# A spectral layer and an FFN in float32: the first DFT of batches 3 to 7 with high and low x stacked on the contraction rows

## The chip, the cores and the metric

One core of a Trainium2 chip runs the whole program. The metric is the device time of one execution in microseconds. The engines are TensorE (PE in the profile, with its weight loads as PEld), VectorE (DVE), ScalarE (ACT), GpSimd (POOL) and SyncE (SP), which issues all DMAs of this kernel in the order of its queue.

## The reference

The input x is 8 x 3008 x 256. Along the sequence of 3008 a real FFT is taken, each frequency is multiplied by a complex 256 x 256 matrix with a bias, real and imaginary parts are shrunk towards zero by 0.01, and the inverse FFT goes back to the sequence. The 24064 rows that result go through an FFN with 2048 hidden units and g = h - tanh(h).

```
X = rfft(x, axis=1);  Xr, Xi = X.real, X.imag
Yr = Xr @ w_r - Xi @ w_i + b_r;  Yi = Xr @ w_i + Xi @ w_r + b_i
Yr, Yi = sign(Y) * max(abs(Y) - 0.01, 0)      # each of the two
y = irfft(Yr + 1j * Yi, n=3008, axis=1).reshape(24064, 256)
h = y @ w_in;  out = (h - tanh(h)) @ w_out
```

## The kernel before

**Accuracy.** A float32 operand is split into a high part, rounded to the format that TensorE multiplies (F32R), and the low remainder. A product is then three matmuls: low matrix by high data, high by high, high by low, added up in one PSUM bank. The high part is a cast on ACT, the low part a subtraction on POOL or DVE (`split_into`, lines 86 to 89; its two operations carry the lines L87 and L88 in the profile).

**The spectral part, batch by batch.** 3008 = 47 x 64, so the FFT falls into two. The *first DFT* is over 47 points for all 64 residues, which are 32 *pairs* of two: a pair has 94 rows (2 x 47) and 256 channels, and the table f1 (94 x 96) holds the 47-point table twice, one block for each residue of the pair. `Forward` loads four pairs, splits two at a time (`split`), multiplies them (`dft`, three matmuls with 94 contraction rows and 512 columns, L216 to L218), copies the bank out (`keep`, L230) and stores four pairs to an intermediate in DRAM (`a_dram`). The *second DFT* (`Spectrum`) reads the intermediate in another order (`load`, tile `at`), transforms it (`dft`), multiplies it with the 256 x 256 matrices (`shared`, `cross`), adds (`join`), shrinks and transforms back (`inverse`, tile `zo`), and stores it to `z_dram`. A `Unit` loads up to four pairs of that (tile `zin`) and makes the last inverse DFT with the table i2, which lies whole in SBUF (L428); its result goes to the tile `raw`, the input of the FFN.

**The FFN.** The tokens go by in 48 chunks (six a batch) of 512 or 480. From chunk 3 on, each chunk is eight `Pair`s of two blocks of 128 hidden units. The first layer is a Strassen-like scheme with seven products of half size, whose operands (t3, b11, t2, b21, t1, b22, t4; tiles y_t, y_b, y_more) are sums and splits made once a chunk on ACT and POOL (`sums`, `operands`). A pair has the PSUM tile H: products in four phases, a sum on DVE between phase 1 and 2 (`u3`, L611) and one after phase 2 (`low_right`, L617), then tanh on ACT (L626), h - tanh(h) on DVE (`g`, L629), the split (L633, L637), and the second layer (`down`, L524).

**Order.** The program is written out by hand: each engine runs its instructions in the order in which the code makes them. The main loop goes over the pairs, two *slots* a pair, sixteen a chunk, 96 a batch. `plan()` puts the spectral steps into slots: `put(slot, rank, fn)`, and in a slot the lower rank goes first. What a step returns is run a little later in the same or the next slot (`run_later`, `run_last`). With zs as the slot of a batch's first chunk, the second DFT of batch b has its twelve steps at zs - 89, zs - 83 and so on, six slots apart, each with its products two, three and seven slots later, and its load seven slots ahead. The sixteen steps of the first DFT go, from batch 2 on, into the calmest slots between zs - 113 and zs - 94 (`calmest`), a place where the second DFT of the batch before has ended and its own has not begun; each step is split one slot ahead. Two PSUM banks (tag `f`) serve all spectral steps in turn, and the tiles of the splits (tags `sp_h`, `sp_l`, two buffers each) serve the first DFT, the second and the shrunk result.

## Time and profile before

| | |
|---|---|
| median of 3 runs | 2632.07 us (2631.01 to 2635.33) |
| the profiled execution | 2638.48 us |
| its span, first to last instruction | 2636.7 us |
| mean granted TensorE clock | 0.995 |
| DMA | 163.88 MB, mean 62 GB/s |

The profile is one execution, 6.4 us above the median. Its page gives the busy time of each engine over the span, the chain of waits that ended last, and the costliest groups of instructions by line, with the mean duration of one and the idle time ahead of it. Stretches, groups, waits and the order in time can be asked of the trace. The steady state begins near 500 us, and a batch then takes 318 us.

### The profile page before, as it was taken

What the parts mean: (1) busy time and instruction counts of PE and PEld (TensorE: products, weight loads), DVE (VectorE), ACT (ScalarE), POOL (GpSimd) and SP (SyncE); (2) the same over time, 40 slices, a digit from 0 to 9 for tenths busy, and PEclk for the clock granted to TensorE, in tenths of its full rate; (3) what the DMA queues carried; (4) which work ended last, traced back from release to release, by engine and by line L of the source; (5) the groups of instructions that cost most, each with busy time, mean ns of one, the idle gap of its engine ahead of it and who ended that gap; (6) DMA issues with size and microseconds to landing.
All of it is one profiled execution on the core that took longest, in us unless ns stands there. A gap on an engine that the chain in (4) does not pass through costs nothing.

```text
span 2636.7 us, 43245 instructions
## 1 busy us (share of the span) xinstructions
PE 2604.5 (99%) x16641; PEld 2344.8 (89%) x16641; DVE 1728.6 (66%) x2612; ACT 1571.5 (60%) x2870; POOL 695.5 (26%) x830
## 2 busy tenths in 40 slices
PE   8999999999999999999999999999999999999999
PEld 6787888899989999899998999999999999999998
DVE  6787775676656667566665667656665667665655
ACT  5555656655576555755666555665556655565655
POOL 0002524322252222412223222332223322221210
PEclk9999999999999999999999999999999999999999
DMA  6520323211131111411114011231112211111000
GB/s 194 153 76 15 112 68 99 66 51 40 47 104 59 48 46 38 119 47 40 46 48 128 29 55 39 80 88 42 42 53 85 69 46 54 36 33 33 16 25 16
DMA packets 104653, 163.88 MB, mean 62 GB/s; under 512 B 8000, under 2 KB 62272, under 8 KB 104352
## 3 DMA queue, kind: packets, MB, share of 16 engines
q1 hardware_dynamic: 104448, 161.13, 20.1%
q8 instruction: 131, 2.15, 0.4%
q14 instruction: 74, 0.61, 0.1%
HBM read 86.13 MB, written 74.97 MB: 61 GB/s over the span
## 4 chain that ended last, share of the span: by engine, by line
PE 92%; issue 2%; POOL 2%; DVE 2%; DMA 1%; ACT 1%; POOLq 0%; SPq 0%; ACTq 0%; DVEq 0%
PE o L524 37%; PE H L595 32%; PE ps_v L289 4%; PE ps_i L428 4%; PE ps_f L262 3%; PE ps_t L289 2%; PE he L500 2%; PE ps_v L371 1%; PE ps_f L218 1%; PE ps_f L216 1%; PE ps_f L217 1%; DVE y L326 1%; PE oe L524 1%; PE ps_i L336 1%; PE ps_i L337 1%
## 5 line engine op out<-in xcount | busy, mean ns | idle before, releaser
L595 PEld LDWEIGHTS H<-y_t,sum 128*128 128x128 f32 x3240 | 531.3, 189 | 86.9 <-POOL y_t L88 1.4
L633 ACT CAST gh<-th 128x1024 fp32r<-128x1024 f32 (+1 forms) x360 | 372.3, 1034 | 362.5 <-DVE th L629 268.0
L524 PE MATMUL o<-gh,wout_l 128*128 128x512 f32 (+1 forms) x1440 | 568.5, 395 | 0.1
L524 PE MATMUL o<-gl,wout_h 128*128 128x512 f32 (+1 forms) x1440 | 560.2, 389 | 0.5 <-DVE gl L637 0.5
L524 PE MATMUL o<-gh,wout_h 128*128 128x512 f32 (+1 forms) x1440 | 559.8, 389 | 0.0
L595 PE MATMUL H<-y_t,sum 128*128 128x256 f32 (+1 forms) x3240 | 551.0, 278 | 1.4 <-ACT ot L535 0.7
L637 DVE TENSOR_TENSOR gl<-th,gh 128x1024 fp32r<-128x1024 f32 (+1 forms) x360 | 441.3, 1226 | 58.1 <-ACT gh L633 54.4
L629 DVE TENSOR_TENSOR th<-H,th 128x1024 f32<-128x1024 f32 (+1 forms) x360 | 429.4, 1193 | 3.8 <-ACT th L626 1.4
L611 DVE TENSOR_TENSOR H<-H,late 128x256 f32<-128x256 f32 (+1 forms) x360 | 153.5, 426 | 417.9 <-PE H L595 373.9
L626 ACT ACTIVATE th<-H 128x1024 f32<-128x1024 f32 (+1 forms) x360 | 364.4, 1012 | 105.5 <-PE H L595 101.9
L524 PEld LDWEIGHTS o<-gl,wout_h 128*128 128x128 f32 x1440 | 270.9, 188 | 55.3 <-DVE gl L637 0.9
L617 DVE TENSOR_TENSOR H<-H,late 128x256 f32<-128x256 f32 (+1 forms) x360 | 153.6, 427 | 248.6 <-PE H L595 241.6
L88 POOL TENSOR_TENSOR z_l<-mn,z_h 128x512 fp32r<-128x512 f32 x84 | 110.7, 1318 | 741.4 <-ACT z_h L87 741.4
L595 PE MATMUL H<-y_b,win_h 128*128 128x256 f32 (+1 forms) x1440 | 286.4, 279 | 0.5
L524 PEld LDWEIGHTS o<-gh,wout_l 128*128 128x128 f32 x1440 | 272.2, 189 | 9.1 <-DVE ot L537 1.1
L524 PEld LDWEIGHTS o<-gh,wout_h 128*128 128x128 f32 x1440 | 271.9, 189 | 6.7
L595 PE MATMUL H<-y_more,win_h 128*128 128x256 f32 (+1 forms) x1440 | 267.4, 279 | 0.4 <-POOL y_more L88 0.4
L603 ACT COPY late<-H 128x256 f32<-128x256 f32 (+1 forms) x360 | 132.8, 369 | 222.1 <-PE H L595 218.3
L595 PEld LDWEIGHTS H<-y_more,win_h 128*128 128x128 f32 x1440 | 220.0, 189 | 5.9 <-POOL y_more L88 0.6
L595 PEld LDWEIGHTS H<-y_b,win_h 128*128 128x128 f32 x1440 | 219.6, 189 | 1.7 <-POOL y_b L88 1.7
L595 PE MATMUL H<-y_more,win_l 128*128 128x256 f32 (+1 forms) x720 | 206.4, 287 | 0.5 <-DVE H L617 0.5
L595 PE MATMUL H<-y_b,win_l 128*128 128x256 f32 (+1 forms) x720 | 200.1, 278 | 0.0
(176 smaller groups left out, 4177.5 us busy)
## 6 DMA issues: line engine op xcount, KB each, us to landing
xt<-in_x SPq DMA_DIRECT2D x64, 384.0 KB, 3.8
at<-a SPq DMA_DIRECT2D x96, 256.0 KB, 3.2
z<-zo SPq DMA_DIRECT2D x96, 256.0 KB, 2.1
a<-st SPq DMA_DIRECT2D x56, 384.0 KB, 3.2
zin<-z SPq DMA_DIRECT2D x49, 384.0 KB, 4.3
out<-ot SPq DMA_DIRECT2D x32, 512.0 KB, 3.1
out<-ot SPq DMA_DIRECT2D x16, 480.0 KB, 3.0
w_raw<-in_moe_w_in SPq DMA_DIRECT2D x8, 512.0 KB, 6.4
```

The costliest lines, as they stand in the source:

```text
L88: rest.tensor_tensor(out=lo, in0=src, in1=hi.bitcast(F32), op=ALU.subtract)
L289: nc.tensor.matmul(dst, lhs[:, t], rhs[:, t, :], start=n == 0, stop=n == 5)
L428: nc.tensor.matmul(ps[:, at + j * 94:at + (j + 1) * 94], self.zt[:, k, t * P:(t + 1) * P], i2t[:, (self.p + k) * 94:(self.p + k + 1) * 94] ...
L524: nc.tensor.matmul(self.o[t][:, :n], lhs[:, f, t * P:(t + 1) * P], rhs, start=f == 0 and k == 0, stop=f == NF - 1 and k == 2,)
L595: nc.tensor.matmul(dst, a, b, start=start and k == 0, stop=k == 2, skip_group_check=True)
L603: nc.scalar.copy(out=self.p7, in_=self.c11)
L611: nc.vector.tensor_tensor(out=self.c21, in0=self.acc, in1=self.p7, op=ALU.add)
L617: nc.vector.tensor_tensor(out=self.c22, in0=self.acc, in1=self.p7, op=ALU.add)
L626: nc.scalar.activation(out=self.th, in_=self.hp[:, :, :n], func=AF.Tanh)
L629: nc.vector.tensor_tensor(out=self.th, in0=self.hp[:, :, :self.n], in1=self.th, op=ALU.subtract)
L633: nc.scalar.copy(out=self.gh, in_=self.th)
L637: nc.vector.tensor_tensor(out=self.gl, in0=self.th, in1=h(self.gh), op=ALU.subtract)
```

## The change

For batches 3 to 7 the first DFT is done by a new class, `Stacked`, on one pair of 512 columns after another. x comes in a second layout, `x_twice`, which the host writes: a pair has both residues side by side (2 x 256 columns), on rows 0 to 46 and again on rows 64 to 110. Both copies are cast on ACT; on rows 64 to 127 the cast is then replaced by the low part, for the first pair of a step on POOL, for the second on DVE. So one operand of 128 rows has high x above and low x below. The table f1s has the high matrix against both, which gives 48 output rows, and the low matrix against high x, which gives 48 more. One matmul a pair does what three did for two pairs, so a step of two pairs has two matmuls into two banks. The two groups of 48 rows are not added in PSUM: they are stored to two intermediates (`a_dram[b][0]` and `[1]`), both are loaded by the second DFT, and POOL adds the second to the first (`fix`) ahead of the transform.

The steps are no longer crowded together: they stand six slots apart, between the steps of the second DFT of the batch before, and the last three four slots apart. A step is split two slots ahead, at the end of the slot.

The table i2 is given up after the first units. Its space in SBUF, a tile named `shared`, then holds two pieces of the table, which each unit loads for itself, two buffers for the second intermediate, and every third load of `x_twice`.

```diff
     f1 = np.zeros((94, 96))
     f1[:47, :48] = one
     f1[47:, 48:] = one
+    f1s = np.zeros((128, 96))
+    f1s[:47, :48] = f1s[:47, 48:] = f1s[64:111, :48] = one
     n1 = np.array([2 * pair + par for par in range(2) for pair in range(NP)])
     th = 2 * np.pi * np.outer(n1, np.arange(128) % 64) / 64
     c, s = np.cos(th).reshape(2, NP, 128), np.sin(th).reshape(2, NP, 128)
...
             i2[par, 0, :, pair, par] = w * np.cos(ps)
             i2[par, 1, :, pair, par] = -w * np.sin(ps)
     i2 = i2.reshape(96, NP * 94)
-    return [np.ascontiguousarray(v, np.float32) for v in (f1, f2, i1, i2)]
+    return [np.ascontiguousarray(v, np.float32) for v in (f1, f1s, f2, i1, i2)]
 
 
 @with_exitstack
-def spectral_ffn(ctx, tc, x, w_r, w_i, b_r, b_i, w_in, w_out, f1, f2, i1, i2, out):
+def spectral_ffn(ctx, tc, x, w_r, w_i, b_r, b_i, w_in, w_out, x_twice, f1, f1s, f2, i1, i2, out):
     nc = tc.nc
     P = 128
     w_in, w_out = w_in.bitcast(U32), w_out.bitcast(U32)
...
     wout_h = const.tile([P, NF, D], F32R, name="wout_h")
     wout_l = const.tile([P, NF, D], F32R, name="wout_l")
 
+    shared, turns = [], {}
+
+    def shared_piece(kind, first, size, bufs):
+        k = turns[kind] = turns.get(kind, -1) + 1
+        lo = first + k % bufs * size
+        return shared[0][:, lo:lo + size]
+
+    def share():
+        shared.append(work.tile([P, NP * 94], F32, name="shared", tag="i2", bufs=1))
+
     def piece(k, shape, dtype, name):
         return work.tile(shape, dtype, name=name, tag=f"sum{k}", bufs=1)
 
...
 
         def load(self):
             if self.ch == 0:
-                a_dram[self.b] = dram.tile([NP, 96, D], F32, name=f"a_{self.b}", tag="a")
+                a_dram[self.b] = dram.tile([2, NP, 96, D], F32, name=f"a_{self.b}", tag="a")
             if self.b == 0 and self.ch // 2 == 1:
                 self.xt = piece(self.ch - 2, [96, XC, D], F32, "xt")
             else:
                 tag = "ot" if self.b == 1 and self.ch in (4, 7) else ("xt", None, ("y0h", "y1h")[self.ch % 2], ("y0l", "y1l")[self.ch % 2])[self.ch // 2 if self.b == 0 else 0]
                 self.xt = work.tile([96, XC, D], F32, name="xt", tag=tag, bufs=2 if tag == "xt" else 1)
-            nc.sync.dma_start(out=self.xt, in_=x[self.b, :, self.ch * XC:(self.ch + 1) * XC, :])
+            nc.sync.dma_start(out=self.xt, in_=x[:, self.b * NP + self.ch * XC:self.b * NP + (self.ch + 1) * XC, :])
 
         def split(self, q, home=None, rest=nc.gpsimd):
             src, name = self.xt[:94, 2 * q:2 * q + 2, :], f"x_{self.b}_{self.ch}_{q}"
...
             copy(out=st[:, p:p + 2, :], in_=self.ps[q][:96].rearrange("p (a d) -> p a d", d=D))
             if p + 2 == n:
                 p = self.ch * XC + 2 * q + 2 - n
-                nc.sync.dma_start(out=a_dram[self.b][p:p + n].rearrange("a p d -> p a d"), in_=st)
+                nc.sync.dma_start(out=a_dram[self.b][0, p:p + n].rearrange("a p d -> p a d"), in_=st)
 
         def part(self, q):
             self.dft(q)
             self.keep(q)
+
+    class Stacked:
+        def __init__(self, b, p):
+            self.b, self.p = b, p
+
+        def load(self):
+            if self.p == 0:
+                a_dram[self.b] = dram.tile([2, NP, 96, D], F32, name=f"a_{self.b}", tag="a")
+            if self.p % 6 == 4:
+                self.xt = shared_piece("x2", 2 * 4 * 94 + 4 * D, 4 * D, 1).rearrange("p (a d) -> p a d", a=2)
+            else:
+                self.xt = work.tile([P, 2, 2 * D], F32, name="x2", tag="xt", bufs=2)
+            nc.sync.dma_start(out=self.xt, in_=x_twice[self.b - 3, :, self.p:self.p + 2, :])
+
+        def split(self):
+            self.x = [work.tile([P, 2 * D], F32R, name=f"x{k}", tag=f"sp_{'hl'[k]}", bufs=2) for k in range(2)]
+            for k in range(2):
+                nc.scalar.copy(out=self.x[k], in_=self.xt[:, k])
+            self.low(0, nc.gpsimd)
+            return [lambda: self.low(1, nc.vector)]
+
+        def low(self, k, engine):
+            v = self.x[k][64:]
+            engine.tensor_tensor(out=v, in0=self.xt[64:, k], in1=h(v), op=ALU.subtract)
+
+        def part(self):
+            ps = [bank("ps_f1") for _ in range(2)]
+            for k in range(2):
+                nc.tensor.matmul(ps[k][:96], f1t[0], self.x[k], start=True, stop=True)
+            st = work.tile([96, 2, 2 * D], F32, name="st", tag="st")
+            for k, copy in enumerate((nc.scalar.copy, nc.vector.tensor_copy)):
+                copy(out=st[:, k], in_=ps[k][:96])
+            src = st.rearrange("r a (g d) -> r (a g) d", d=D)
+            for v in range(2):
+                dst = a_dram[self.b][v, self.p:self.p + 2].rearrange("a (g r) d -> r (a g) d", g=2)
+                nc.sync.dma_start(out=dst, in_=src[48 * v:48 * v + 48])
+
+    f1t = []
+
+    def stacked_table():
+        raw = work.tile([P, 96], F32, name="f1s_f", tag="tmp", bufs=4)
+        hi = work.tile([P, 48], F32R, name="f1s_h", tag="tmp", bufs=4)
+        nc.sync.dma_start(out=raw, in_=f1s)
+        t = work.tile([P, 96], F32R, name="f1s", tag="f1s", bufs=1)
+        nc.vector.tensor_copy(out=t[:, :48], in_=raw[:, :48])
+        nc.vector.tensor_copy(out=hi, in_=raw[:, 48:])
+        nc.vector.tensor_tensor(out=t[:, 48:], in0=raw[:, 48:], in1=hi.bitcast(F32), op=ALU.subtract)
+        f1t.append(t)
 
     def rows(t, jp):
         return t.rearrange("a (g j) d -> a g (j d)", j=NJ)[:, :, 2 * jp * D:(2 * jp + 2) * D]
...
             if self.jp == 0:
                 z_dram[self.b] = dram.tile([NP, 96, D], F32, name=f"z_{self.b}", tag="z")
             self.at = load.tile([P, 2, D], F32, name="at", tag="at", bufs=3)
-            nc.sync.dma_start(out=self.at.rearrange("p j d -> p (j d)"), in_=rows(a_dram[self.b], self.jp))
+            nc.sync.dma_start(out=self.at.rearrange("p j d -> p (j d)"), in_=rows(a_dram[self.b][0], self.jp))
+            if self.b > 2:
+                self.al = shared_piece("al", 2 * 4 * 94, 2 * D, 2)
+                nc.sync.dma_start(out=self.al, in_=rows(a_dram[self.b][1], self.jp))
+
+        def fix(self):
+            at = self.at.rearrange("p j d -> p (j d)")
+            nc.gpsimd.tensor_tensor(out=at, in0=at, in1=self.al, op=ALU.add)
 
         def transform(self):
             ps = self.ps = bank("ps_f2")
...
                 tag = ("y0h", "y0l")[Unit.turn % 2]
                 Unit.turn += 1
                 self.zt = work.tile([96, 4, D], F32, name="zin", tag=tag, bufs=1)
+                self.table = shared_piece("i2", 0, 4 * 94, 2)[:96, :self.n * 94]
+                nc.sync.dma_start(out=self.table, in_=i2[:, self.p * 94:(self.p + self.n) * 94])
             else:
                 self.zt = piece(self.home, [96, 4, D], F32, "zin")
+                self.table = i2t[:, self.p * 94:(self.p + self.n) * 94]
             nc.sync.dma_start(out=self.zt[:, :self.n, :], in_=z_dram[self.b][self.p:self.p + self.n].rearrange("a p d -> p a d"))
 
         def time(self, t):
...
             for j, k in enumerate(which or range(self.n)):
                 nc.tensor.matmul(
                     ps[:, at + j * 94:at + (j + 1) * 94], self.zt[:, k, t * P:(t + 1) * P],
-                    i2t[:, (self.p + k) * 94:(self.p + k + 1) * 94], start=True, stop=True,
+                    self.table[:, k * 94:(k + 1) * 94], start=True, stop=True,
                 )
 
         def pieces(self, k=0, n=None):
...
             s = Spectrum(b, jp)
             k = at + jp * each
             put(max(k - ahead, earliest), 0, s.load)
+            if b > 2:
+                put(k - 3, 0.7, s.fix)
             for slot, rank, fn, us in (
                 (k, 6, s.dft, 1.8), (k + shared, 4, s.shared, 0.7), (k + cross, 3, s.cross, 1.4),
                 (k + shrink, 2, lambda s=s: [s.shrink], 0.3), (k + inverse, 2.5, s.inverse, 0.7),
...
             if shared == cross:
                 busy(k + shared, 9.0)
 
-    def plan_forward(f, q, slot):
-        put(slot - 1, 0.5, f.split, q)
-        put(slot, 7, f.part, q)
+    def plan_forward(f, slot, *q):
+        if len(q):
+            put(slot - 1, 0.5, f.split, *q)
+        else:
+            put(slot - 2, 8.5, f.split)
+        put(slot, 7, f.part, *q)
         busy(slot, 0.8)
         busy(slot - 1, 0.1)
 
...
         for p, at in enumerate((36, 40, 46, 50)):
             for k in range(4):
                 put(at + k, 9, weight_step, p, k)
+        put(38, 0, share)
+        put(39, 9, stacked_table)
         put(40, 0, first_spares)
         put(42, 0, operand_tiles)
         put(45, 0, more_operand_tiles)
...
             f = following[ch]
             put((40, 41, 44, 47, 48, 49)[k], 0, f.load)
             for q in range(XC // 2):
-                plan_forward(f, q, 47 + k)
+                plan_forward(f, 47 + k, q)
         plan_spectrum(1, 56, 2, (1, 1, 2, 4), 5, 53)
         for b in range(2, B):
             zs = zero_slot(b * WB_N)
             plan_spectrum(b, zs - 89, 6, (2, 3, 4, 7), 7, zs - 92)
         for b in range(2, B):
             zs = zero_slot(b * WB_N)
-            at = calmest(zs - 113, zs - 94, NP // 2, 0.8)
-            for ch in range(NP // XC):
+            if b == 2:
+                at = calmest(zs - 113, zs - 94, NP // 2, 0.8)
+            else:
+                at = [zs - 184] + [zs - 180 + 6 * k for k in range(12)] + [zs - 111 + 4 * (k + 1) for k in range(3)]
+                for k in at:
+                    busy(k, 0.8)
+            for ch in range(NP // XC if b == 2 else 0):
                 f = Forward(b, ch)
                 put(at[2 * ch] - 5, 0, f.load)
                 for q in range(XC // 2):
-                    plan_forward(f, q, at[2 * ch + q])
+                    plan_forward(f, at[2 * ch + q], q)
+            for k in range(NP // 2 if b > 2 else 0):
+                f = Stacked(b, 2 * k)
+                put(max(at[k] - 6, at[k - 3] - 1 if k > 2 else 0), 0.6, f.load)
+                plan_forward(f, at[k])
         for c in range(FIRST + 1, NCH):
             b, i = c // WB_N, c % WB_N
             lo, hi = (-(-(begin[c + k] - b * S) // 94) if c + k < NCH and i + k < WB_N else NP for k in range(2))
...
         nc.gpsimd.memset(rebias, -896.0)
         idle(16)
         units = [WholeSpectrum(0, jp) for jp in range(NJ // 2)]
-        i2t = const.tile([96, NP * 94], F32, name="i2")
+        i2t = work.tile([96, NP * 94], F32, name="i2", tag="i2", bufs=1)
         lin = []
         NU = len(units)
         homes = ["y0h", "y0l", "y1h", "y1l", "y0h", "y0l"] + ["xt"] * 4 + [f"sum{k}" for k in (3, 4, 5, 0, 1, 2)]
...
     nc = bacc.Bacc("TRN2", target_bir_lowering=False, num_devices=1, dynamic_dma_scratch_size=1024)
     time, _ = index_maps()
     given = {n: np.ascontiguousarray(inputs[n]) for n in _INS}
-    xs = given["x"][:, time.reshape(-1), :].reshape(B, NP, 2 * 47, D)
-    given["x"] = np.zeros((B, 96, NP, D), np.float32)
-    given["x"][:, :94] = xs.transpose(0, 2, 1, 3)
-    given |= dict(zip(("f1", "f2", "i1", "i2"), dft_constants()))
+    xs = given["x"][:, time.reshape(-1), :].reshape(B, NP, 2, 47, D)
+    given["x"] = np.zeros((96, 3 * NP, D), np.float32)
+    given["x"][:94] = xs[:3].transpose(2, 3, 0, 1, 4).reshape(94, 3 * NP, D)
+    given["x_twice"] = np.zeros((B - 3, 2, 64, NP, 2, D), np.float32)
+    given["x_twice"][:, :, :47] = xs[3:, None].transpose(0, 1, 4, 2, 3, 5)
+    given["x_twice"] = given["x_twice"].reshape(B - 3, 128, NP, 2 * D)
+    given |= dict(zip(("f1", "f1s", "f2", "i1", "i2"), dft_constants()))
     arrays, args = {}, []
     for name in ("moe_w_in", "moe_w_out"):
         given[name] = given[name].view(np.int64)
...
+    given["x"] = np.zeros((96, 3 * NP, D), np.float32)
+    given["x"][:94] = xs[:3].transpose(2, 3, 0, 1, 4).reshape(94, 3 * NP, D)
+    given["x_twice"] = np.zeros((B - 3, 2, 64, NP, 2, D), np.float32)
+    given["x_twice"][:, :, :47] = xs[3:, None].transpose(0, 1, 4, 2, 3, 5)
+    given["x_twice"] = given["x_twice"].reshape(B - 3, 128, NP, 2 * D)
```

## The prediction

> **What bounds the kernel now.** I read the page's first lines and its chain of waits, then the busy time by stretches of one batch, then who TensorE waits for, and last the order of time around one step that the change touches.
>
> ```profile
> span 2636.7 us, 43245 instructions
> PE 2604.5 (99%) x16641; PEld 2344.8 (89%) x16641; DVE 1728.6 (66%) x2612; ACT 1571.5 (60%) x2870; POOL 695.5 (26%) x830
> PE 92%; issue 2%; POOL 2%; DVE 2%; DMA 1%; ACT 1%; POOLq 0%; SPq 0%; ACTq 0%; DVEq 0%
> 1026.60:1344.80 318.20, 317.97 (x2111) 290.60 (x2111) 206.35 (x306) 193.73 (x355) 94.14 (x111) 1.00 0.20 60
> ```
>
> The last row is one stretch, one batch of the steady state: its length, then the busy time of PE, PEld, DVE, ACT and POOL, the granted clock, the DMA share and GB/s. TensorE is idle for 0.2 of 318.2 us, and the clock is full. The other engines are busy for 65%, 61% and 30% of it. A busy PE is not yet a full PE, since a matmul's row overlaps the next one's, so I looked at the start times:
>
> ```profile
> 1059.42 0.39 PE L216 MATMUL ps_f<-x_h,f_l 94*96 94x512 f32 x1
> 1059.65 0.40 PE L217 MATMUL ps_f<-x_h,f_h 94*96 94x512 f32 x1
> 1059.89 0.39 PE L218 MATMUL ps_f<-x_l,f_h 94*96 94x512 f32 x1
> 1060.12 0.38 PE L524 MATMUL o<-gh,wout_l 128*128 128x480 f32 x1
> 1003.11 0.40 PE L524 MATMUL o<-gh,wout_l 128*128 128x512 f32 x1
> 1003.36 0.39 PE L524 MATMUL o<-gh,wout_h 128*128 128x512 f32 x1
> 1003.59 0.40 PE L524 MATMUL o<-gl,wout_h 128*128 128x512 f32 x1
> 1003.82 0.50 PE L595 MATMUL H<-y_t,sum 128*128 128x240 f32 x3
> ```
>
> Start time, duration, what. Each lasts 0.39 us but the next starts 0.23 us after it. The three matmuls of the first DFT take 1060.12 - 1059.42 = 0.70 us, so 0.233 each. The last four rows show that a contraction over 128 rows costs the same as one over 94: (1003.82 - 1003.11)/3 = 0.237. The price of a matmul here is its 512 columns. So in the steady state TensorE is the bound, and a matmul taken out is worth 0.233 us, if nothing else becomes late.
>
> ```profile
> PE ps_i L428 <- DMA zin<-z: 3.6, 2, 2.3
> PE H L595 <- POOL y_t L88: 0.6, 4, 0.2
> PE ps_f L218 <- POOL x_l L88: 0.9, 2, 0.5
> ```
>
> Waits of TensorE, total, times and longest. The largest is a DMA at the start of the program; those for POOL sum to about a microsecond in the whole run.
>
> **The change, part by part.** *Matmuls removed.*
>
> ```profile
> L216 PE MATMUL ps_f<-x_h,f_l 94*96 94x512 f32 x112 | 45.4, 406 | 1.4 <-DVE y L326 0.8 <-ACT x_h L87 0.6
> ```
>
> x112 over seven batches is 16 steps a batch. Five batches change, so 80 steps go from three matmuls of 512 columns to two: 80 fewer, 80 x 0.233 = 18.6 us. A step of the old kernel, TensorE's rows (x_1_0 is a group of two sequence pairs, h and l its parts):
>
> ```order
> L216 MATMUL ps_f_7167<-x_1_0_h,f_l 96x512
> L217 MATMUL ps_f_7167<-x_1_0_h,f_h 96x512
> L218 MATMUL ps_f_7167<-x_1_0_l,f_h 96x512
> L524 MATMUL o_7173<-gh,wout_l 128x480
> L524 MATMUL o_7173<-gh,wout_h 128x480
> ```
>
> The three products into one bank (ps_f) are followed at once by the FFN's second layer. A step of the new kernel, TensorE's rows in the middle of batch 5's first DFT:
>
> ```order
> L278 MATMUL ps_f_12920<-x_12849,f1s 96x512
> L278 MATMUL ps_f_12921<-x_12850,f1s 96x512
> L665 MATMUL H_2043<-y_more,win_l 128x256
> L665 MATMUL H_2043<-y_more,win_h 128x256 x2
> L665 MATMUL H_2043<-y_more,win_l 128x256
> ```
>
> Two products, each into a bank of its own, now stand ahead of the FFN's first layer, in the one slot of six that the second DFT and its products leave free.
>
> The Trainium skill prices this differently: TensorE: Matmul & The Clock Gate, section Back-to-back issue gap, gives a sustained spacing of about 131 ns for 512 columns. By that the gain would be an estimated 10.5 us. The rows above say 233 ns here, and they decide.
>
> *Work added beside it.* Nearest rows for one step's new operations:
>
> ```profile
> L88 DVE TENSOR_TENSOR x_l<-xt,x_h 94x512 fp32r<-94x512 f32 x4 | 2.7, 684 | 0.4 <-ACT x_h L87 0.3
> L230 DVE COPY st<-ps_f 96x512 f32<-96x512 f32 x7 | 4.8, 681 | 0.0
> L87 ACT CAST z_h<-mn 128x512 fp32r<-128x512 f32 x84 | 52.3, 623 | 2.5 <-DVE mn L315 2.4
> L88 POOL TENSOR_TENSOR z_l<-mn,z_h 128x512 fp32r<-128x512 f32 x84 | 110.7, 1318 | 741.4 <-ACT z_h L87 741.4
> L88 POOL TENSOR_TENSOR x_l<-xt,x_h 94x512 fp32r<-94x512 f32 x108 | 140.1, 1300 | 164.5 <-ACT x_h L87 102.4 <-PE H L595 59.3 <-PE ps_f L218 1.5
> ```
>
> DVE gets one subtraction and one copy a step, 0.684 + 0.681 = 1.37 us, so 206.35 + 16 x 1.37 = 228 us of 314 in a batch. ACT gets one more cast, 0.62 us: 204 us. POOL keeps one subtraction a step and gets 12 additions a batch at 1.32: 110 us. Nobody is near full. If none of it were covered, it would cost 80 x 1.37 = 109 us for DVE, 80 x 0.62 = 50 for ACT, 60 x 1.32 = 79 for POOL; with full cover, 0. Which end holds depends on the one place where they are tight, the slot of the cross products, into which the splits now go. DVE's rows there in the old kernel:
>
> ```order
> L300 TENSOR_TENSOR tb<-ps_t_9551,bias 128x512
> L637 TENSOR_TENSOR gl<-th,gh 128x1024
> L326 TENSOR_TENSOR y<-tb,ps_v 64x256 x4
> L611 TENSOR_TENSOR H_2035<-H_2035,late 128x256
> L629 TENSOR_TENSOR th<-H_2034,th 128x1024
> ```
>
> The four additions of y are followed by the sum in H (L611) and the subtraction from tanh (L629). The same place of the new kernel, where x_12850 is the second pair of a split:
>
> ```order
> L367 TENSOR_TENSOR tb<-ps_t_12802,bias 128x512
> L707 TENSOR_TENSOR gl<-th,gh 128x1024
> L393 TENSOR_TENSOR y<-tb,ps_v 64x256 x4
> L273 TENSOR_TENSOR x_12850<-x_12688,x_12850 64x512
> L681 TENSOR_TENSOR H_2043<-H_2043,late 128x256
> L699 TENSOR_TENSOR th<-H_2042,th 128x1024
> ```
>
> The low part of the second pair now stands ahead of the sum in H (L611, now L681), for which TensorE's product with t1 waits, and ahead of L629 (now L699), which must have read H before TensorE opens it again. In time, before:
>
> ```profile
> 924.89 0.36 ACT L604 COPY H<-H 128x256 f32<-128x256 f32 x1
> 926.61 1.03 ACT L626 ACTIVATE th<-H 128x1024 f32<-128x1024 f32 x1 [1.37 <-PE H L595]
> 925.90 1.72 DVE L326 TENSOR_TENSOR y<-tb,ps_v 64x256 f32<-64x256 f32 x4 [0.67 <-PE ps_v L289]
> 928.07 0.43 DVE L611 TENSOR_TENSOR H<-H,late 128x256 f32<-128x256 f32 x1 [0.45 <-PE H L595]
> 928.53 1.23 DVE L629 TENSOR_TENSOR th<-H,th 128x1024 f32<-128x1024 f32 x1
> 929.17 0.52 PE L595 MATMUL H<-y_t,sum 128*128 128x256 f32 x3
> 930.23 0.51 PE L595 MATMUL H<-y_t,sum 128*128 128x256 f32 x3
> 919.00 0.74 POOL L88 TENSOR_TENSOR s_l<-xi,s_h 128x256 fp32r<-128x256 f32 x1 [6.42 <-ACT s_h L87]
> 932.50 1.30 POOL L88 TENSOR_TENSOR z_l<-mn,z_h 128x512 fp32r<-128x512 f32 x1 [12.77 <-ACT z_h L87]
> ```
>
> - ACT idles 1.37 us ahead of tanh. Two casts, 1.25 us, fit.
> - DVE idles 0.45 us ahead of L611. The subtraction, 0.684, exceeds it by 0.23, so L611 and L629 end 0.23 later. L611 ends at 928.50 and the product with t1 starts at 929.17, a slack of 0.67; L629 ends at 929.76 and TensorE opens H at 930.23, a slack of 0.47. It is covered with 0.24 left.
> - POOL idles 12.77 us between its two rows. The addition to the operand (1.32) follows s_l at once, since its operands are loaded four slots before it; the low part (1.30) follows the first cast and ends near 927.2, before DVE begins the other.
>
> The copy out of the second bank (0.681) falls in the free slot, which TensorE has lengthened by 2 x 0.233. I take 0 for all three, the end nearest to these rows.
>
> *DMA.*
>
> ```profile
> xt<-in_x SPq DMA_DIRECT2D x64, 384.0 KB, 3.8
> at<-a SPq DMA_DIRECT2D x96, 256.0 KB, 3.2
> a<-st SPq DMA_DIRECT2D x56, 384.0 KB, 3.2
> zin<-z SPq DMA_DIRECT2D x49, 384.0 KB, 4.3
> 919.85 0.38 SPq L253 DMA_DIRECT2D at<-a  x1
> ```
>
> A batch now loads 16 x 512 KB of x instead of 8 x 384, stores and reloads twice the intermediate, and fetches a table of up to 141 KB per unit: some 13.6 MB more. To the 60 GB/s x 318 us = 19 MB of before that makes 33 MB, about 103 GB/s and a share of 0.34. An issue holds SP 0.38 us; some eight in six slots (20 us, a slot being 318.2/96 = 3.3) do not fill it. The tightest turn is the first load of a batch's second DFT, seven slots (23 us) after the last step: copy, store (3.2), load (3.2) make under 10. POOL's first addition may stand some 4 us for that load; in its queue no operand of the FFN is behind it. Value 0, except at the one DMA wait above, 2.3 us long: the table is issued ahead of zin and its 141 KB may take from 0 to 4.3 x 141/384 + 0.38 = 2.0 us of it. I take 0.5.
>
> *Once only.* The stacked table is loaded and split in slot 39, three short DVE operations. DVE would stall for the landing if SP issued it late, at most the 4.3 us above; SP has nothing else to wait for there, so 0.
>
> Sum: -18.6 + 0.5 = -18.1 us. Against the profiled execution, span 2636.7 and time 2638.48, that is 2618.6 and 2620.4. The three timed runs have a median of 2632.07, 6.4 below the profiled one, and I carry the difference over: 2614.
>
> **Rivals.** *POOL holds DVE up, and the kernel is slower.*
>
> ```profile
> L637 DVE TENSOR_TENSOR gl<-th,gh x360: 1143/1216/2191, 269.4 to 2628.6; 128x1024 fp32r<-128x1024 f32 x116, 128x960 fp32r<-128x960 f32 x64
> L315 DVE SCALAR_TENSOR_TENSOR mn<-y,mn x84: 691/693/1115, 310.6 to 2322.7; 128x512 f32<-128x512 f32 x84
> ```
>
> Minimum, median, maximum. A DVE operation with both inputs in SBUF takes up to 0.975 us longer than its median when a POOL operation runs beside it. The new subtraction is of that kind, and POOL's half of the same split lasts 1.30. If the two meet in every slot, L611 is late by 0.684 + 0.975 - 0.45 = 1.21, and TensorE waits 1.21 - 0.47 = 0.74 in some 60 slots: 44 us, 2614 + 44 = 2658. It outweighs the gain from a wait of 18.6/60 = 0.31 on, a lateness of 0.78. For it: both halves are released by neighbouring casts. Against it: by the rows DVE is in its four additions until 927.62, when POOL is done. The Trainium skill, SBUF — State Buffer, section Who interferes with whom, states this as an exclusive lock that the first instruction keeps to its end; the maximum of 2191 agrees.
>
> *Half of it is given back.* The subtraction is only stretched to the 1.115 of L315: late by 0.67, a wait of 0.2 in 60 slots, 12 us: 2626.
>
> *TensorE's time is not freed.* The stacked matmul could cost more than 0.233, or the freed time turn into waits as long: 2632. The rows with 128 contraction rows and the 0.2 us of idle time speak against it.
>
> **How the numbers follow.** Forecast 0.80, half given back 0.07, nothing freed 0.06, slower 0.07. A difference below 0.2%, about 5 us, could not be told from none. So faster 0.87 (the first two), same 0.06, slower 0.07. The forecast's own bounds are the DMA's 0 to 2.0 us, the once-only 4.3, and a few us less if the waits of the old crowded stage vanish. To hold 8 in 10 the range goes from 2608 to 2624, which leaves out the last two cases and part of the second.
>
> **What would show it.** Right: some 16561 matmuls, a batch of about 314.5 us with PE still idle for under 0.5, L278 matmuls starting 0.23 apart. Wrong: waits of TensorE for L681 or for L699 in the slot of the cross products, about sixty times; a low part on DVE far above 0.7 us; POOL additions that wait for a DMA with operands of the FFN behind them; a wait over 3 us for the table or for zin near 440 us.

## The result, and the profile after

The changed kernel takes 2616.02 us (median of six runs, 2615.15 to 2617.88) against 2633.07 for the kernel before beside it. The ratio is 0.9934, with a 95% interval of 0.9921 to 0.9947: 17.05 us less by the medians, 14 to 21 by the interval. The forecast was 2614, or 18.1 us less, with a range of 2608 to 2624.

The first lines of the page of the changed kernel, with its chain of waits by engine and its DMA total:

```profile
span 2613.4 us, 44156 instructions
PE 2583.2 (99%) x16561; PEld 2323.5 (89%) x16561; DVE 1840.4 (70%) x2775; ACT 1617.5 (62%) x2950; POOL 777.6 (30%) x890
PE 94%; DVE 2%; DMA 1%; issue 1%; POOL 1%; ACT 1%; SPq 0%; POOLq 0%; ACTq 0%; DVEq 0%
DMA packets 147621, 230.14 MB, mean 88 GB/s; under 512 B 15952, under 2 KB 91152, under 8 KB 147312
```

TensorE has 16561 matmuls, 80 fewer, and is still busy for 99% of the span. DVE has 112 us more work in all, ACT 46 and POOL 82, and the program is shorter all the same. The DMA total is 230.14 - 163.88 = 66 MB larger.

One batch of the steady state in the changed kernel, with the columns of the row that the prediction shows (length, PE, PEld, DVE, ACT, POOL, clock, DMA share, GB/s):

```profile
1016.20:1330.80 314.60, 314.54 (x2095) 287.20 (x2094) 228.51 (x338) 202.90 (x372) 110.82 (x124) 1.00 0.34 101
```

A batch took 318.20 us and takes 314.60. Both are windows with ends at whole tenths. From the first matmul of one second DFT (L262, now L329) to that of the next, a batch has a mean of 318.07 us before and 314.54 in the changed kernel, and its five batches agree to 0.2 us: 3.5 less, in five batches 17.7. TensorE is idle for 0.06 us of the stretch.

The groups of the changed operations (busy time, mean ns of one, idle time of the engine ahead of them):

```profile
L278 PE MATMUL ps_f<-x,f1s 128*96 128x512 f32 x160 | 50.3, 396 | 0.0
L281 DVE COPY st<-ps_f 96x512 f32<-96x512 f32 x80 | 54.4, 680 | 0.0
L273 DVE TENSOR_TENSOR x<-x,x 64x512 fp32r<-64x512 f32 x55 | 49.4, 898 | 5.2 <-ACT x L267 4.9
L273 DVE TENSOR_TENSOR x<-shared,x 64x512 fp32r<-64x512 f32 x25 | 20.3, 812 | 1.2 <-ACT x L267 1.2
L320 POOL TENSOR_TENSOR at<-at,shared 128x512 f32<-128x512 f32 x60 | 77.8, 1296 | 71.1 <-DMA shared<-a 71.1
```

The copy and POOL's addition last about what the rows before had said (681 and 1318 ns). DVE's subtraction does not: 69.7 us for 80, a mean of 871 ns where 684 was put in. The 71.1 us for which POOL stands until the second intermediate lands are five waits, one ahead of the first addition of each batch, of 13.8 to 15.4 us; the other 55 additions do not wait.

The slot of the cross products in the changed kernel, in time (start, duration, what; a selection of rows by engine):

```profile
1296.06 1.72 DVE L393 TENSOR_TENSOR y<-tb,ps_v 64x256 f32<-64x256 f32 x4 [0.67 <-PE ps_v L356]
1297.70 1.00 DVE L273 TENSOR_TENSOR x<-x,x 64x512 fp32r<-64x512 f32 x1
1298.73 0.43 DVE L681 TENSOR_TENSOR H<-H,late 128x256 f32<-128x256 f32 x1
1299.19 1.22 DVE L699 TENSOR_TENSOR th<-H,th 128x1024 f32<-128x1024 f32 x1
1296.07 1.29 POOL L273 TENSOR_TENSOR x<-x,x 64x512 fp32r<-64x512 f32 x1 [4.91 <-issue]
1297.44 0.70 POOL L620 TENSOR_TENSOR late<-raw 128x240 f32<-128x240 f32 x1
1298.23 1.04 POOL L620 TENSOR_TENSOR raw<-raw 128x240 f32<-128x240 f32 x1
1299.93 0.39 PE L594 MATMUL o<-gh,wout_h 128*128 128x512 f32 x1
1300.16 0.40 PE L594 MATMUL o<-gl,wout_h 128*128 128x512 f32 x1
1300.47 0.63 PE L665 MATMUL H<-y_t,sum 128*128 128x256 f32 x3
1301.28 0.63 PE L278 MATMUL ps_f<-x,f1s 128*96 128x512 f32 x2
1301.75 0.28 PE L665 MATMUL H<-y_more,win_l 128*128 128x256 f32 x1
```

POOL's own half of the split (L273) is done before DVE begins, as forecast. But POOL goes on with sums for the next chunk (L620), and DVE's subtraction then lasts 1.00 us in place of 0.684. It ends at 1298.70, 0.56 after the end of POOL's first sum (1297.44 + 0.70 = 1298.14), which was running when it began. L699 ends at 1300.41 where TensorE would have opened H at 1300.16 + 0.23 = 1300.39; it opens it at 1300.47, 0.08 late. That is what the margin looks like when it is used up. The last two rows show the price of the stacked matmuls: two of them in 1301.75 - 1301.28 = 0.47 us, 0.235 each.

TensorE's largest waits in the changed kernel, the one for zin among them (total, times, longest):

```profile
PE ps_i L498 <- DMA zin<-z: 2.3, 2, 2.0
PE ps_f L329 <- DMA at<-a: 3.9, 1, 3.9
PE ps_i L403 <- DVE y L393: 4.0, 7, 0.6
```

The wait for zin did not grow (3.6 before); the other two were there before, with 4.1 and 4.0. No wait for L681 or L699 has a row, and the old one for y_t from POOL is gone. Delays as short as the 0.08 above do not show as waits, since a matmul's row of 0.39 us covers the next start 0.23 later and up to 0.16 more. Summed from TensorE's start times (what each lies above the usual spacing of its shape) they are 2.75 us in a batch before and 3.2 after, so some 0.4 us a batch is given back that way.

### The profile page after: what moved, and what is told of

Read it like the earlier page. It is cut to its first block, busy times and chain, and to the rows that moved or that the text cites. A ratio compares the mean times of both kernels' runs of the same rounds, so it can differ in the third digit from the quotient of the medians.

```text
span 2613.4 us, 44156 instructions
## 1 busy us (share of the span) xinstructions
PE 2583.2 (99%) x16561; PEld 2323.5 (89%) x16561; DVE 1840.4 (70%) x2775; ACT 1617.5 (62%) x2950; POOL 777.6 (30%) x890
## 2 busy tenths in 40 slices
DMA packets 147621, 230.14 MB, mean 88 GB/s; under 512 B 15952, under 2 KB 91152, under 8 KB 147312
## 4 chain that ended last, share of the span: by engine, by line
PE 94%; DVE 2%; DMA 1%; issue 1%; POOL 1%; ACT 1%; SPq 0%; POOLq 0%; ACTq 0%; DVEq 0%
PE o L594 38%; PE H L665 33%; PE ps_v L356 4%; PE ps_i L498 4%; PE ps_f L329 3%; PE he L570 2%; PE ps_t L356 2%; PE ps_f L278 1%; PE ps_v L438 1%; PE oe L594 1%; DVE y L393 1%; PE ps_i L403 1%; PE ps_i L404 1%; PE ps_i L405 1%; DMA a<-st 1%
## 5 line engine op out<-in xcount | busy, mean ns | idle before, releaser
L699 DVE TENSOR_TENSOR th<-H,th 128x1024 f32<-128x1024 f32 (+1 forms) x360 | 429.8, 1194 | 4.9 <-ACT th L696 2.6
L681 DVE TENSOR_TENSOR H<-H,late 128x256 f32<-128x256 f32 (+1 forms) x360 | 153.6, 427 | 321.7 <-PE H L665 282.2
L687 DVE TENSOR_TENSOR H<-H,late 128x256 f32<-128x256 f32 (+1 forms) x360 | 153.3, 426 | 220.3 <-PE H L665 211.6
L393 DVE TENSOR_TENSOR y<-tb,ps_v 64x256 f32<-64x256 f32 x384 | 160.7, 419 | 56.2 <-PE ps_v L356 45.0
```

What stands on the lines that cost most here:

```text
L393: nc.vector.tensor_tensor(out=y[ri * 64:(ri + 1) * 64, jj, :], in0=common(jj, ri), in1=self.vv[jj * 64:(jj + 1) * 64, ri * D:(ri + 1) * D] ...
L681: nc.vector.tensor_tensor(out=self.c21, in0=self.acc, in1=self.p7, op=ALU.add)
L687: nc.vector.tensor_tensor(out=self.c22, in0=self.acc, in1=self.p7, op=ALU.add)
L699: nc.vector.tensor_tensor(out=self.th, in0=self.hp[:, :, :self.n], in1=self.th, op=ALU.subtract)
```

## The experiments

The times of one kernel's runs lie 1 to 9 us apart here. The traces have a finer measure, the length of a batch as above. Each row is the mean of the same five batches, which agree to 0.3 us, in one execution (not all on one chip):

| kernel | us a batch |
|---|---|
| before | 318.07 |
| before, steps spread | 318.53 |
| changed | 314.54 |
| changed, one matmul more in each step | 318.11 |
| changed, subtraction twice | 323.43 |
| changed, subtraction later | 314.00 |
| changed, subtraction later and twice | 319.95 |
| changed, both low parts on POOL | 314.90 |
| changed, no additions | 314.44 |

### What a matmul is worth: one more in each step

```diff
-            for k in range(2):
-                nc.tensor.matmul(ps[k][:96], f1t[0], self.x[k], start=True, stop=True)
+            for k, of in ((0, 1), (0, 0), (1, 1)):
+                nc.tensor.matmul(ps[k][:96], f1t[0], self.x[of], start=True, stop=True)
```

> The changed kernel with a third matmul of 512 columns put back into each of the 80 steps (a product whose bank is overwritten by the next). My theory: TensorE is the bound, so each costs 0.233 us: 2616.0 + 18.6 = 2634.6 us (2632 to 2637). Rival, that the time of TensorE is partly hidden by waits in these slots: 2616 to 2628 us.

Measured: 2636.01 us, within the expected 2632 to 2637, ratio to the kernel before 1.0003 (0.9995 to 1.0012). Against the changed kernel that is 20.0 us by the medians and 18 by the ratios, for 80 matmuls 0.23 to 0.25 us each. By the batches it is 318.11 - 314.54 = 3.57 us for 16, or 0.22 each. The group of the three in its trace:

```profile
L278 PE MATMUL ps_f<-x,f1s 128*96 128x512 f32 x240 | 68.2, 392 | 0.0
```

240 matmuls are three for each of 80 steps, with no idle time of TensorE ahead of them. As many as were removed are put back, and the whole gain is gone: what the change saves is the matmuls.

### Is the gain from the spreading? The old steps at the new places

The kernel before, with the sixteen steps of batches 3 to 7 put where the changed kernel has them:

```diff
-            at = calmest(zs - 113, zs - 94, NP // 2, 0.8)
+            if b == 2:
+                at = calmest(zs - 113, zs - 94, NP // 2, 0.8)
+            else:
+                at = [zs - 184] + [zs - 180 + 6 * k for k in range(12)] + [zs - 111 + 4 * (k + 1) for k in range(3)]
+                for k in at:
+                    busy(k, 0.8)
```

> The kernel before, with the first DFT's steps of batches 3 to 7 spread over the same slots as in the change, still three matmuls a step. My theory: the gain comes from the 80 matmuls alone, so this is 2633 us (2630 to 2635), the time of before; the crowded stage gives back at most the 0.35 us a batch that TensorE waits in it. Rival, that the spreading is what pays: 2616 to 2626 us.

Measured: 2636.44 us, ratio 1.0011 (1.0002 to 1.0019). The same stretch as in the kernel before, then the wait for POOL's split of the FFN operand, which had 0.6 us in all there:

```profile
1026.60:1344.80 318.20, 317.84 (x2108) 290.55 (x2107) 209.31 (x306) 193.12 (x356) 93.54 (x111) 1.00 0.20 60
```

```profile
PE H L595 <- POOL y_t L88: 1.7, 6, 0.3
```

TensorE's idle time in the stretch is 0.36 us where it was 0.23. The time lies 1.4 us above the expected range (2630 to 2635). Spreading by itself gains nothing. It costs 2 us by the medians, which an interval that begins at 1.0002 barely tells from nothing, and 318.53 - 318.07 = 0.46 us by the batch.

### What the spreading is good for: the stacked steps crowded

The changed kernel, with the steps of batches 3 to 7 in the calmest of the twenty slots again:

```diff
-            if b == 2:
-                at = calmest(zs - 113, zs - 94, NP // 2, 0.8)
-            else:
-                at = [zs - 184] + [zs - 180 + 6 * k for k in range(12)] + [zs - 111 + 4 * (k + 1) for k in range(3)]
...
+            at = calmest(zs - 113, zs - 94, NP // 2, 0.8)
```

> The changed kernel with its stacked steps put back into the calmest slots between zs - 113 and zs - 94. My theory: the matmuls go all the same, 18.6 us, but 16 steps in 20 slots with two casts, a subtraction and a copy more than fit beside the FFN bring waits of some 0.1 to 0.5 us a step, so 2618 to 2630 us. Rival, that spreading is what pays: 2630 us or more. If it is 2616, spreading does nothing at all.

Measured: 2685.38 us, ratio 1.0188 (1.0174 to 1.0201). That is 69 us over the changed kernel, 14 a batch, and slower than the kernel before: far over the 2618 to 2630 that were expected. TensorE's largest waits in the whole run, then stretches inside one crowded place (columns as above):

```profile
PE ps_i L498 <- ACT st L281: 16.7, 15, 2.3
PE H L665 <- DVE H L681: 15.9, 25, 1.0
PE o L594 <- DVE ot L607: 6.1, 5, 1.2
```

```profile
1076.00:1086.00 10.00, 7.11 (x40) 5.00 (x38) 8.93 (x10) 8.05 (x16) 3.85 (x3) 1.00 1.00 331
1086.00:1096.00 10.00, 9.56 (x43) 8.54 (x44) 4.65 (x6) 3.94 (x8) 1.28 (x1) 0.66 0.59 166
```

In the first stretch the DMA share is 1.00, at 331 GB/s, and TensorE is busy for 7.11 of 10 us with 40 matmuls; in the second the granted clock is 0.66. The chain of waits at this place, in time, shows what the copies out of the banks (L281) stand for (its rows of issue, of 0.02 to 0.44 us, and of the semaphores are left out):

```profile
1069.13 5.70 DMA a<-st
1074.93 0.04 ACT st L281
1075.41 1.15 ACT x L267 x2
1076.77 5.38 DMA a<-st
```

Two stores are on the path, 5.70 and 5.38 us long, where the median store of 192 KB lands in 3.0 us in the changed kernel and in 3.6 in this one. ACT's copy waits for the buffer that the first store frees, and the casts of the next step come after it in ACT's queue. Three causes are possible: stores that land late, DVE with more to do in the same few slots, and two banks that come free late.

### Which of them: DVE relieved, or one store taken away

First the crowded steps with both low parts on POOL:

```diff
-            return [lambda: self.low(1, nc.vector)]
+            self.low(1, nc.gpsimd)
```

> The crowded kernel (2685 us) with both low parts on POOL. If DVE and what POOL takes from it cause the crowding's 69 us, 80 x 0.9 us less on DVE bring most of them back: 2625 to 2655 us. If DMA or the two PSUM banks do: 2675 to 2690 us.

Measured: 2697.29 us, ratio 1.0241 (1.0227 to 1.0255), 12 us slower still and above both expected ranges. ACT's wait for the stores, in the stretch from 1040 to 1130 us, and the wait of TensorE over the whole run:

```profile
ACT st L281 <- DMA a<-st: 8.1, 3, 5.4
```

```profile
PE ps_f L278 <- ACT st L281: 17.7, 7, 3.8
PE H L665 <- POOL y_t L90: 5.0, 5, 1.0
```

DVE's sum in H is no longer among the largest waits; the copy for the banks takes its place, and POOL appears. So this does not measure what DVE's work costs in the crowd: it takes that away and brings other waits, and a lower clock. The mean granted clock is 0.986 in this trace, 0.993 in the crowded one and 0.997 in the changed kernel.

Then the crowded steps with the second intermediate neither stored nor loaded nor added:

```diff
-            for v in range(2):
+            for v in range(1):
...
-            if self.b > 2:
-                self.al = shared_piece("al", 2 * 4 * 94, 2 * D, 2)
-                nc.sync.dma_start(out=self.al, in_=rows(a_dram[self.b][1], self.jp))
...
-                put(k - 3, 0.7, s.fix)
+                pass
```

> The crowded kernel with the second intermediate neither stored nor loaded nor added (the low-matrix part is left out of the result). That takes 192 of 896 KB a step out of a stage in which the DMA engines are busy for 0.80 of the time, at times for all of it. If DMA causes the crowding's 69 us, a good part comes back: 2635 to 2665 us. If DVE or the banks do: 2675 to 2690 us.

Measured: 2671.26 us, ratio 1.0146 (1.0132 to 1.016): 14 us less than crowded with both stores, and still 55 over the changed kernel: between the two expected ranges. The store's wait on ACT over the same 90 us is 2.8 us in place of 5.3, and DVE's late sum is there almost as before:

```profile
PE ps_i L495 <- ACT st L281: 13.7, 15, 2.1
PE H L662 <- DVE H L678: 13.2, 22, 1.0
```

Taking away the transfers of the second intermediate (and the additions, which cost nothing where the steps are spread, as shown below) brings back a fifth of the loss.

Part of these differences is the clock. An estimate from the traces: what the granted clock lacks of 1 in each stretch of 10 us, times 10 us, summed from 700 to 2300 us, is 10 us in the crowded kernel, 29 with both low parts on POOL, 2 with one store less, and 0 in the changed kernel. So the clock may make up 10 of the 69 us, all of the 12 us by which the kernel with both low parts on POOL is slower, and 8 of the 14 that one store less gains. Without it, each of the two would lie some 6 to 7 us below the crowded kernel, and neither late stores nor DVE's work is shown to be the main cause. The rest of the loss, the two banks and the loads of x among its possible causes, stays undivided.

### How much room DVE has: the subtraction twice

The changed kernel, with DVE's subtraction done a second time at the same place, its result not used:

```diff
-            return [lambda: self.low(1, nc.vector)]
+            return [lambda: self.low(1, nc.vector), self.again]
+
+        def again(self):
+            v = self.xt[64:, 1]
+            nc.vector.tensor_tensor(out=v, in0=v, in1=h(self.x[1][64:]), op=ALU.subtract)
```

> The changed kernel with the subtraction on DVE done a second time, 0.68 us more in DVE's queue ahead of the sum in H in each of 80 steps, 60 of them in a slot with cross products. My theory: the slack there, 0.47 us less the 0.23 already taken, is 0.24 us or less, so TensorE waits 0.4 to 0.6 us in some 60 slots: 2616 + 24 to 36 = 2640 to 2652 us. Rival, that DVE's lateness has no part in the time: 2616 us.

Measured: 2663.9 us, ratio 1.0112 (1.0098 to 1.0126): 48 us over the changed kernel, 0.60 us for each of 80 steps, above what was expected (2640 to 2652). TensorE's waits in it, then the second subtraction's durations (minimum, median, maximum):

```profile
PE H L669 <- DVE H L685: 21.9, 25, 1.0
PE o L598 <- DVE gl L711: 3.2, 11, 0.5
```

```profile
L273 DVE TENSOR_TENSOR x<-x,x x55: 689/1045/1122, 493.9 to 2079.3; 64x512 f32<-64x512 f32 x55
L273 DVE TENSOR_TENSOR shared<-shared,x x25: 689/689/690, 529.1 to 2068.3; 64x512 f32<-64x512 f32 x25
```

The wait that the prediction's first rival named, for the sum in H, is there. The expectation had put both subtractions at 0.684. In this trace the first has a mean of 0.87 us over the 80 steps and the second of 0.84 (0.911 for the 55, 0.689 for the 25). Together they exceed the 0.45 us for which DVE was idle and the slack of 0.47 by 0.79, and 0.79 us in the sixty slots of the cross products would be 47 us, near the 48 measured.

### Another place for it: behind the sum in H

The changed kernel, with the subtraction one slot later, behind L681 and L699 and ahead of L687, first once:

```diff
-            return [lambda: self.low(1, nc.vector)]
+            return []
+
+        def second(self):
+            self.low(1, nc.vector)
...
+            put(slot - 1, 1, f.second)
```

> The changed kernel with DVE's subtraction moved one slot on, behind the sum in H and the subtraction from tanh, ahead of the second sum in H (L687). In the trace of the changed kernel that sum ends some 1.0 to 1.2 us ahead of TensorE's use in these slots. My theory: the few waits that the subtraction makes now, about 0.5 us a batch, go: 2613 to 2616 us. Rival, that it is as bad ahead of the second sum: 2616 to 2620 us.

Measured: 2615.53 us, ratio 0.9927 (0.9913 to 0.994), as expected (2613 to 2616), but not told apart from the changed kernel's 0.9934. The batch tells them apart: 314.00 us in place of 314.54, and the short delays of TensorE are 2.7 us in it where they were 3.2.

The same with the subtraction twice (`again` as above):

```diff
         def second(self):
             self.low(1, nc.vector)
+            self.again()
```

> The same with the subtraction done twice, as in the kernel that took 2664 us with it ahead of the first sum. My theory: the place sets the price, and here 1.0 to 1.2 us of slack stand against 1.4 to 1.7 us, so waits of 0.2 to 0.5 us in 60 slots: 2626 to 2646 us. Rival, that 0.68 us more on DVE costs the same anywhere: 2660 to 2668 us.

Measured: 2644.01 us, ratio 1.0036 (1.0023 to 1.0048), within the expected 2626 to 2646: 20 us less than twice at the old place. Its largest wait of TensorE:

```profile
PE H L673 <- DVE H L695: 9.2, 15, 0.8
```

So the later place has more room, 20/80 = 0.25 us a step more. For one subtraction it buys about 0.5 us a batch, some 2.7 us in five, since one costs little more where it is.

### Both low parts on POOL, and no additions

The changed kernel with the second low part on POOL too:

```diff
-            return [lambda: self.low(1, nc.vector)]
+            self.low(1, nc.gpsimd)
```

> The changed kernel with both low parts of a step on POOL, none on DVE. In the changed kernel 40 of the 80 subtractions on DVE are held up by a POOL operation. My theory: DVE's lateness costs TensorE only some 0.5 us a batch, so 2613 to 2616 us. Rival: 1.29 us more of POOL ahead of the chunk's operands make TensorE wait for y_more or y_t, some 0.3 us in two chunks of six: 2618 to 2622 us.

Measured: 2618.92 us, ratio 0.9944 (0.9931 to 0.9958). The wait for y_t from POOL is back:

```profile
PE H L665 <- POOL y_t L90: 1.7, 5, 0.3
```

That is the rival's range (2618 to 2622), not that of the theory (2613 to 2616). By the medians the kernel is 2.9 us slower, though the two intervals overlap; by the batch it is 0.36 us slower, 1.8 in five. So it cannot show that DVE's subtraction costs nothing, only that POOL in its place costs more. The wait for y_t alone does not explain it, since the kernel with the later subtraction has 1.3 us of it and is no slower.

The changed kernel without POOL's sixty additions, so that the low-matrix part is missing from the result while it is still stored and loaded:

```diff
-                put(k - 3, 0.7, s.fix)
+                pass
```

> The changed kernel without POOL's 60 additions of the second intermediate (the low-matrix part is left out of the result; it is still stored and loaded). My theory: the additions run in POOL's idle time, so 2616 us (2614.5 to 2617.5). Rival, that they hold DVE or the chunk's operands up: 2608 to 2613 us.

Measured: 2616.87 us, ratio 0.9936 (0.9924 to 0.9949), and 314.44 us a batch in place of 314.54. The additions, 78 us of POOL's time, cost no more than 0.1 us a batch, and neither do the 71 us that POOL stands waiting ahead of them.

## Why the prediction was right, point by point

**The bound.** TensorE was the bound and still is: idle for 0.2 of 318.2 us in a batch before, 0.06 of 314.6 after.

**The price of a matmul.** 0.233 us was forecast from start times, and the independence of 94 or 128 rows with it. The stacked ones follow each other at 0.235, and 80 more of them cost 0.23 to 0.25 each by the times, 0.22 by the batches. By the 131 ns of the Trainium skill, TensorE: Matmul & The Clock Gate, section Back-to-back issue gap, putting them back would have cost an estimated 10.5 us; the run gave 18 to 20. The term of 18.6 us holds, and of it 17.7 is seen in the batches.

**Busy times and DMA.** DVE 228, ACT 204, POOL 110 and a DMA share of 0.34 at 103 GB/s were forecast; 228.5, 202.9, 110.8, 0.34 and 101 came out.

**The additions at 0.** Right, shown by leaving them out. The 4 us that POOL might stand for the first load of a batch was too small: it stood 13.8 to 15.4 us in each of the five. The sum from the last step, "copy, store (3.2), load (3.2) make under 10", had no wait of SP's queue in it. In the batch of the stretch shown, SP stood 11.7 us at a store of the output ahead of this load, until DVE's copy for it (L607) was done; the load went out at 1106.55 and POOL's addition began at 1110.47. In the other four SP stood 11.3 to 12.2 us at the same store. Nothing behind the additions made TensorE wait.

**The subtraction at 0, with 0.24 us left.** The sum was nearly right, one step of its working was not. By the start times, 40 of the 80 subtractions begin while POOL works. That POOL's half ends "before DVE begins the other" holds for 65 steps; in the other 15 POOL is still at its own half of the split. The other 25 of the forty meet the sums for the next chunk (L620), which the prediction did not have on its list. The rows of the changed kernel by duration:

```profile
L273 DVE TENSOR_TENSOR x<-x,x x55: 684/884/1422, 487.7 to 2029.8; 64x512 fp32r<-64x512 f32 x55
L273 DVE TENSOR_TENSOR x<-shared,x x25: 684/685/1319, 522.0 to 2018.8; 64x512 fp32r<-64x512 f32 x25
```

The mechanism of the slower rival is thus there, with up to 1.422 us, but not in every slot. Over all steps it adds 0.871 - 0.684 = 0.19 us on average. In the sixty steps right behind the cross products, the place of the prediction's sum, 25 are held, with 0.12 us on average over the sixty and 0.35 at most: the 0.24 us cover most of it, and the 0.4 us of short delays a batch fits what they do not cover. The longest ones, 1.32 to 1.42 us, are ten of the twenty steps at other places. That there was enough slack is in part luck, since L620 was not counted. Doubling the subtraction shows how near the edge lay: 0.60 us a step lost. The rival would have needed the two to meet in every slot at the full length, and they met in 25 of the sixty at less.

**The wait for zin, +0.5.** It did not come: 2.3 us in place of 3.6. This lies below the 0 to 2.0 us that were given, and is less than can be measured in a whole run.

**The three other cases.** "Half of it is given back", 12 us in sixty slots, would be 2.4 us a batch: the batch is 3.5 us shorter, and the short delays grew by 0.4. "TensorE's time is not freed" falls with the batch of 314.5 us. "A few us less if the waits of the old crowded stage vanish" was no gain: the old steps at the new places are no faster.

**What the prediction did not say.** It priced the places of the steps only as they stand. That the change needs them is what the crowded run shows: the same operations, in the old twenty slots, lose 69 us and the gain with it. A stacked step moves 512 + 2 x 192 = 896 KB where an old one moved half of 384 twice, and its cast, copy and subtraction come on top; six slots apart this is a DMA share of 0.34 over a batch, in the crowd one of 1.00 over 10 us. Why the crowd costs 69 us is only in part known, as said above.

## What to carry to other kernels

Where TensorE never idles, price a matmul by the spacing of starts in the trace and look at columns, not at contraction rows: here filling idle rows took matmuls out at no cost on that engine. Work added to other engines costs little as long as its place in the queue has slack ahead of the next thing TensorE waits for, so compare its duration with that slack, at the longest it takes beside the other engine's instructions, those of other stages too. When a gain or a loss is under the scatter of whole times, measure a period that repeats in the trace. When a step gets heavier in transfers and copies, spread the steps: the average load of a batch says nothing of a crowd of sixteen.

## What the runs showed of the hardware that was not expected

- DVE's subtraction from two SBUF operands, 684 ns at its shortest, took up to 1422 beside POOL, and 884 in the median of the 55 of the commoner form. In all 40 that began while a POOL instruction ran, it ended 0.55 us after the end of that instruction (0.546 to 0.552); in the other 40 it took 684 to 690 ns. So its length is what POOL had left, plus 0.55. The Trainium skill, SBUF — State Buffer, section Who interferes with whom, describes an exclusive lock that the first instruction keeps to its end, which agrees with it.
- In the crowded kernel the granted clock fell to 0.66 for the 10 us after a stretch in which TensorE was busy for 7.11 of 10 us. From 1089.0 to 1092.8 us matmuls of 480 columns start 0.40 to 0.42 us apart, where 0.22 is usual. Some 10 of the 69 us may be due to the slower clock, by the estimate above; it was not measured apart.
- In the crowded kernel two stores of 192 KB took 5.7 and 5.4 us, in stretches of 10 us with a DMA share of 0.86 (1066 to 1076 us) and 1.00 (331 GB/s). The median of such a store is 3.0 us in the changed kernel.
